# Main-loop matmuls of an attention block issued as pairs of 64-row halves with swapped PSUM banks

## The chip, the cores and the metric

The kernel runs on one core of a Trainium2 chip. The metric is device time in microseconds (us), the median of several executions. The profile of a kernel is one execution; "L426" is line 426 of that kernel, so that the same code has other line numbers in the changed kernel. Engines: PE is TensorE's matmul, PEld its weight load, DVE is VectorE, ACT ScalarE. PSUM is the memory that TensorE writes its results to; "evacuation" is their copying out of it by DVE or ACT. Matmul ends are modelled and some matmul records are missing (15,453 of them beside 15,729 weight loads in the page before the change), so I work with start-to-start times of matmuls that are both there.

## The reference

```python
x = A_x                                   # 2048 x 640, bf16
xn = layernorm(x)
q = (xn @ wq) -> 32 heads of 192          # per head 2048 x 192
scores = q @ k_cache^T * 192**-0.5        # 2048 x 2048 per head
o = softmax(scores) @ v_cache             # 2048 x 192 per head
s = concat(o) @ wo                        # 2048 x 640
g = silu(swiglu(xn, w1, w3, w2))
return x + s * g
```

## The kernel before

It records its operations in program order, finds the dependencies from named keys, and emits each engine's list with semaphore waits. After LayerNorm, the gated MLP and the first Q projection comes the main loop: 512 steps `n`, one for each head `h`, 512 queries `c` and quarter `qd` of the keys. A step computes scores S for 512 keys, takes their exp, multiplies the previous step's result P by V (PV, summed up as O), and in most steps does one "filler": a piece of the Q projection for the next pair of heads, or of the output projection Wo for the last pair. A head's 192 features are split into 128 (`KT0`, `QT0`) and 64 (`KT1`, `QT1`); the 64-row matmuls of even and odd keys use different halves of the array's rows (in the trace the two start 3 to 4 ns apart).

PSUM is four slots of two banks. `O_ps` is slot 3; S takes two of the other three slots, the filler the third, in rotation. The code is shortened; `...` stands for what is cut.

```python
def emit_S(h, c, qd):
    ss = [slot(), slot()]
    for jj in range(2):
        for par in range(2):            # 128 rows
            matmul(ps[ss[jj]][:, par*512:(par+1)*512], KT0[:, hs, par, ...], QT0[:, q4, ...], start=True, stop=False)
    for jj in range(2):
        for par in range(2):            # 64 rows
            rows = slice(64 * par, 64 * par + 64)
            matmul(ps[ss[jj]][:, par*512:(par+1)*512], KT1[rows, hs, par, ...], QT1[rows, q4, ...], start=False, stop=True)

def emit_PV(h, c, qd):                  # 128 rows, 16 matmuls of 193 columns
    for t in range(4):
        for kk in range(4):
            matmul(O_ps[:, t, 0:193], P_sb[:, pb, jj, par, t*128:(t+1)*128], V_sb[:, hs, 2*qd+jj, par, 0:193], ...)

def qproj1(m, c, engs=("dve",), nrot=3):        # the 64 last features of two heads: "second part"
    s = slot(nrot)
    ...                                          # five 128-row matmuls into ps[s][:, 0:512]
    for hh in range(2):
        for half in range(2):                    # each 64 rows twice, for both halves of the array
            evac_copy(engs[hh % len(engs)], QT1[64*half:64*half+64, h % 4, c*512:(c+1)*512],
                      dst[64*hh:64*hh+64, :], ...)
...
for n in range(total):
    emit_S(h, c, qd); emit_exp(h, c, qd)
    if n >= 1:
        emit_PV(...)                             # of step n - 1
        if k % 4 == 3: unit_tail(k // 4)         # O: reciprocal and scaling on DVE
    for fn in fl[i]: fn()                        # filler
```

## Time and profile before

Median 2116.6 us (2115.5 to 2117.9, 4 runs). From the page of the profile: the span, the busy time of PE (us, share of the span, instructions), and the chain of work that ended last.

```profile
span 2115.0 us, 34282 instructions
...
PE 2028.4 (96%) x15453; PEld 1192.0 (56%) x15729; DVE 714.2 (34%) x1301; ACT 1061.0 (50%) x1128; POOL 126.9 (6%) x155
...
PE 94%; DVE 2%; DMA 2%; issue 1%; ACT 1%; SPq 0%; another core or an unknown queue 0%; DVEq 0%
```

TensorE is the bottleneck by all of these lines. What it does with its time stands in the groups of the page: line, engine, operation, names, shape, count, then busy us and mean ns of one.

```profile
L455 PE MATMUL ps<-V_sb,P_sb 128*128 128x193 bf16 x8192 | 771.7, 248 | 0.0
L426 PE MATMUL ps<-QT,KT 128*128 128x512 bf16 x2030 | 522.7, 379 | 3.1 <-ACT P_sb L444 1.2
L385 DVE CAST QT<-ps 64x512 bf16<-64x512 f32 x368 | 253.7, 689 | 616.2 <-PE ps L392 396.6
L434 PE MATMUL ps<-QT,KT 64*128 64x512 bf16 x2048 | 310.1, 381 | 0.0
```

The L385 group mixes shapes: 248 of its 368 copies have 64 rows, 120 have 128. The mean ns is the life of one matmul, and lives overlap. The records of single matmuls show the rate: where nothing holds them up, 512-column matmuls start every 216 ns and 193-column ones every 83 ns. One step in order of time (start us, us, engine, line; brackets give the idle time before and what ended it), first PE, then the weight loads:

```profile
1000.30 1.03 PE L426 MATMUL ps<-QT,KT 128*128 128x512 bf16 x4
1001.26 0.60 PE L434 MATMUL ps<-QT,KT 64*128 64x512 bf16 x4
1001.80 1.51 PE L455 MATMUL ps<-V_sb,P_sb 128*128 128x193 bf16 x16
```

```profile
1001.26 0.11 PEld L434 LDWEIGHTS ps<-QT,KT 64*128 64x128 bf16 x4 [0.42 <-issue]
1001.79 1.28 PEld L455 LDWEIGHTS ps<-V_sb,P_sb 128*128 128x128 bf16 x16 [0.42 <-issue]
```

Four 128-row matmuls should be followed after 4 x 0.216 = 0.86 us; the 64-row ones come after 0.96. Two 64-row pairs should take 0.43 us; PV comes after 0.54. And the loads (94 ns each for the 64-row matmuls, 98 for PV), which elsewhere are hidden under the matmul before, stand still until then. The waits view has it in total (engine, line, what it waited for: us in total, times, longest us):

```profile
PEld ps L434 <- issue: 217.0, 512, 0.4
PEld ps L455 <- issue: 165.0, 389, 0.4
...
PEld ps L485 <- DVE QT L385: 15.5, 56, 0.3
PE ps L485 <- DVE rall L468: 15.4, 56, 0.3
```

The totals are idle time of the weight load, about 0.42 us each; TensorE itself loses 96 and 93 ns. Of the loads of L455, 122 more stand under DVE's names in this view, 109 of them with 46.2 us; the matmuls there are late by the same amount.

### The profile page before, as it was taken

The page shows a single profiled execution, that of the slowest core. Times are in us where ns is not written, and L with a number is a line of the kernel's source. Part 1 is how long each engine was busy: PE and PEld are TensorE (multiplying, and loading weights), DVE is VectorE, ACT ScalarE, POOL GpSimd, SP SyncE. Part 2 cuts the span into 40 slices and gives each one's busy share as a digit, 9 for nine tenths or more (in the row PEclk, how much of TensorE's full clock was granted, in tenths as well). Part 3 has the DMA queues.
Part 4 walks back from the last instruction along what each step waited for, and adds up shares of the span by engine and source line. Part 5 has one row for each costly group of instructions (what it writes and reads, how often), then busy time and mean ns, then how long its engine had stood idle before and what let it go on. Part 6 is the DMA issues. An engine that isn't in the chain of part 4 may idle for free.

```text
span 2115.0 us, 34282 instructions
## 1 busy us (share of the span) xinstructions
PE 2028.4 (96%) x15453; PEld 1192.0 (56%) x15729; DVE 714.2 (34%) x1301; ACT 1061.0 (50%) x1128; POOL 126.9 (6%) x155
## 2 busy tenths in 40 slices
PE   4899999999999999999999999999999999999995
PEld 2444555555555555555555555555555655555563
DVE  4321223333333333333332333323333233332335
ACT  3322655555555555555555555555555555555552
POOL 2000100010101000010101000010101010000000
PEclk9999999999999999999999999999999999999998
DMA  9000032232313222232323112232323222222313
GB/s 235 10 1 1 25 70 50 51 69 43 77 36 71 34 42 58 51 69 43 77 39 82 36 42 43 52 68 51 69 43 77 36 57 43 44 52 51 72 24 96
DMA packets 260586, 115.70 MB, mean 55 GB/s; under 512 B 238544, under 2 KB 250320, under 8 KB 260432
## 3 DMA queue, kind: packets, MB, share of 16 engines
q1 hardware_dynamic: 247488, 70.54, 17.6%
q0 software_dynamic: 12944, 42.87, 7.6%
q8 instruction: 125, 2.05, 0.4%
q14 instruction: 29, 0.24, 0.0%
HBM read 52.04 MB, written 2.62 MB: 26 GB/s over the span
## 4 chain that ended last, share of the span: by engine, by line
PE 94%; DVE 2%; DMA 2%; issue 1%; ACT 1%; SPq 0%; another core or an unknown queue 0%; DVEq 0%
PE ps L455 34%; PE ps L426 21%; PE ps L434 13%; PE ps L485 9%; PE ps L392 6%; PE ps L357 5%; PE ps L403 3%; PE ps L373 2%; DMA w_sb<-in_B_w_dram 1%; DMA x_sb<-in_A_x_dram 1%; DVE rall L468 1%; DVE fin_sb L500 0%; DVE s_acc L493 0%; PE ps L340 0%; DVE o_sb L503 0%
## 5 line engine op out<-in xcount | busy, mean ns | idle before, releaser
L444 ACT ACTIVATE P_sb<-ps 128x1024 bf16<-128x1024 f32 x1024 | 992.3, 1021 | 871.0 <-PE ps L434 870.9
L455 PEld LDWEIGHTS ps<-V_sb,P_sb 128*128 128x128 bf16 x8192 | 655.7, 98 | 216.8 <-issue 165.0
L455 PE MATMUL ps<-V_sb,P_sb 128*128 128x193 bf16 x8192 | 771.7, 248 | 0.0
L426 PE MATMUL ps<-QT,KT 128*128 128x512 bf16 x2030 | 522.7, 379 | 3.1 <-ACT P_sb L444 1.2
L385 DVE CAST QT<-ps 64x512 bf16<-64x512 f32 x368 | 253.7, 689 | 616.2 <-PE ps L392 396.6
L493 DVE TENSOR_TENSOR s_acc<-s_acc,ps 128x640 f32<-128x640 f32 x240 | 196.5, 819 | 487.7 <-PE ps L485 484.9
L434 PE MATMUL ps<-QT,KT 64*128 64x512 bf16 x2048 | 310.1, 381 | 0.0
L426 PEld LDWEIGHTS ps<-QT,KT 128*128 128x128 bf16 x2048 | 188.3, 98 | 195.9 <-ACT P_sb L444 1.7
L485 PE MATMUL ps<-wo_sb,OT_sb 128*128 128x128 bf16 (+1 forms) x1298 | 200.1, 286 | 26.4 <-DVE rall L468 15.4
L434 PEld LDWEIGHTS ps<-QT,KT 64*128 64x128 bf16 x2048 | 58.3, 94 | 217.0 <-issue 217.0
L485 PEld LDWEIGHTS ps<-wo_sb,OT_sb 128*128 128x128 bf16 x1536 | 121.5, 98 | 78.9 <-DVE QT L385 15.5
L392 PE MATMUL ps<-xnT,wq_sb 128*128 128x512 bf16 x639 | 158.5, 379 | 0.1
L470 DVE TENSOR_TENSOR O_sb<-ps,rall 128x384 bf16<-128x384 f32 x256 | 142.8, 558 | 9.1 <-DVE rall L468 0.3
L357 PE MATMUL ps<-xnT,w_sb 128*128 128x512 bf16 x470 | 111.1, 396 | 8.9 <-DMA w_sb<-in_B_w_dram 8.4
L289 POOL DMA_DIRECT2D V_sb<-in_A_v_cache_dram x64 | 56.7, 890 | 876.4 <-PE ps L455 876.4
L392 PEld LDWEIGHTS ps<-xnT,wq_sb 128*128 128x128 bf16 x640 | 60.8, 98 | 47.1
L357 PEld LDWEIGHTS ps<-xnT,w_sb 128*128 128x128 bf16 x480 | 48.2, 101 | 68.7 <-issue 12.8
L403 PE MATMUL ps<-xnT,wq_sb 128*128 128x512 bf16 x319 | 79.5, 379 | 0.1
L468 DVE RECIPROCAL rall<-ps 128x2 f32<-128x2 f32 x256 | 42.3, 165 | 103.3 <-PE ps L455 101.4
L364 DVE TENSOR_TENSOR hT_sb<-sil_sb,ps 128x512 bf16<-128x512 bf16 x48 | 32.7, 681 | 122.9 <-ACT sil_sb L362 122.9
L362 ACT ACTIVATE sil_sb<-ps 128x512 bf16<-128x512 f32 x48 | 28.7, 597 | 86.3 <-PE ps L357 81.3
L283 POOL DMA_DIRECT2D wo_sb<-in_A_wo_dram x16 | 12.3, 766 | 706.2 <-PE ps L485 706.2
(40 smaller groups left out, 290.2 us busy)
## 6 DMA issues: line engine op xcount, KB each, us to landing
V_sb<-in_A_v_cache_dram POOLq DMA_DIRECT2D x64, 384.0 KB, 4.9
wo_sb<-in_A_wo_dram POOLq DMA_DIRECT2D x16, 480.0 KB, 4.2
wq_sb<-in_A_wq_dram POOLq DMA_DIRECT2D x32, 160.0 KB, 3.6
w_sb<-in_B_w_dram SPq DMA_DIRECT2D x8, 480.0 KB, 11.5
x_sb<-in_A_x_dram SPq DMA_DIRECT2D x16, 160.0 KB, 4.9
wq_sb<-in_A_wq_dram POOLq DMA_DIRECT2D x32, 80.0 KB, 3.5
x_sb<-in_A_x_dram SPq DMA_DIRECT2D x4, 640.0 KB, 5.2
out_dram<-o_sb SPq DMA_DIRECT2D x16, 160.0 KB, 1.8
```

The source lines that it names most:

```text
L357: op("pe", lambda e, ct=ct, dst=dst, wt=wt: e.matmul(dst, wt[:, ct, ft * P:(ft + 1) * P], xnT[:, ct, qc * 512:(qc + 1) * 512], start=(ct = ...
L385: op("dve", lambda e: e.tensor_copy(dst, src), r=r, **{mode: w})
L392: op("pe", lambda e, ct=ct: e.matmul(dst, wq_sb[:, m % 2, ct, hh * P:(hh + 1) * P], xnT[:, ct, c * 512:(c + 1) * 512], start=(ct == 0), st ...
L403: op("pe", lambda e, ct=ct: e.matmul(dst, wq_sb[:, m % 2, ct, 2 * P:3 * P], xnT[:, ct, c * 512:(c + 1) * 512], start=(ct == 0), stop=(ct = ...
L426: op("pe", lambda e, jj=jj, j=j, par=par: e.matmul(ps[ss[jj]][:, par * 512:(par + 1) * 512], KT0[:, hs, par, j * P:(j + 1) * P], QT0[:, q4 ...
L434: op("pe", lambda e, jj=jj, j=j, par=par, rows=rows: e.matmul(ps[ss[jj]][:, par * 512:(par + 1) * 512], KT1[rows, hs, par, j * P:(j + 1) * P],
L444: op("act", lambda e, jj=jj, s=s: e.activation(P_sb[:, pb, jj, :, :], ps[s][:, :].rearrange("p (a b) -> p a b", a=2), ACT.Exp, scale=scale ...
L455: op("pe", lambda e, t=t, kk=kk, jj=jj, par=par, first=first: e.matmul(O_ps[:, t, 0:Dh + 1], P_sb[:, pb, jj, par, t * P:(t + 1) * P], V_sb ...
L468: op("dve", lambda e, rr=rr, t0=t0: e.reciprocal(rr, O_ps[:, t0:t0 + 2, Dh:Dh + 1]), r=[("O", b)], w=[("rall", b)])
L470: op("dve", lambda e, rr=rr, t0=t0: e.tensor_tensor(O_sb[:, c, t0:t0 + 2, hh * Dh:(hh + 1) * Dh], O_ps[:, t0:t0 + 2, 0:Dh], rr.to_broadcas ...
L485: op("pe", lambda e, f=f, a=a, b=b: e.matmul(ps[s][:, a:b], OT_sb[:, c, t * 3 + f, :], wo_sb[:, m % 2, f, a:b], start=(f == 0), stop=(f == ...
L493: op("dve", lambda e: e.tensor_tensor(s_acc[:, qt, :], s_acc[:, qt, :], ps[s][:, 0:D], op=ALU.add), r=skeys(s) + [("acc", qt)], w=[("acc", ...
```

## The change

Every main-loop matmul becomes two of 64 rows, one in each half of the array's rows (`k` = 0, 1). The two halves of a pair run at the same time and write different banks `b`; in a second phase they swap banks, so that each bank gets both halves. The intent is to do away with the changes between 128-row and 64-row matmuls. So that both halves never write one bank at once, a recorded dependency makes TensorE wait on its own semaphore before a half writes a bank that the other half wrote last. To give these waits time, the phases of S, PV and filler are interleaved. A second-part Q job now covers 1024 queries, and Q jobs may span two steps, after a fixed pattern.

```diff
+        if tile is not None:
+            bank, k = tile
+            d = self.last_in_bank.get((bank, 1 - k))
+            if d is not None:
+                deps[d.pos] = d
+            self.last_in_bank[(bank, k)] = o
...
-        def qproj0(...)
-        def qproj1(...)
+        def q_phase(kind, m, c, s, phase):
+            for ct in range(NCT):
+                for k in range(2):
+                    b = k if phase == 0 else 1 - k
+                    matmul(ps[s][:, b*512:(b+1)*512], wq_sb[hrows(k), ...], xnT[hrows(k), ct, cc*512:(cc+1)*512],
+                           start=first, stop=..., tile=((s, b), k))
+        def q_evac(kind, m, c, s, engs=("dve", "dve")):
+            ...
+                    evac_copy(engs[hh], QT1[hrows(half), h4 + hh, c * 512:(c + 2) * 512], ps[s][hrows(hh), :], ...)
...
+            for par0 in range(2):            # S, pairs 1 to 4
+                for jj in range(2):
+                    steps.append([(jj, par0, KT0, QT0, 0, par0 == 0), (jj, 1 - par0, KT0, QT0, 1, par0 == 0)])
             for jj in range(2):              # S, pairs 5 and 6
+                steps.append([(jj, 0, KT1, QT1, 0, False), (jj, 1, KT1, QT1, 1, False)])
...
+        PATTERN = "W01WW01WW01.WW.W"         # W: Wo job, 0 and 1: phases of a Q job, '.': no filler
...
-            emit_S(h, c, qd)
-            emit_exp(h, c, qd)
-                emit_PV(...)
-            for fn in fl[i]: fn()
+            steps = emit_S(h, c, qd)
+            cut = 6 if (f1[i] or n == 0) else 4
+            for st in steps[:cut]: st()
+            if cut == 6: emit_exp(h, c, qd)
+            emit_PV(..., 0)                  # first phase
+            for st in steps[cut:]: st()
+            if cut < 6: emit_exp(h, c, qd)
+            if f1[i]: f1[i]()
+            emit_PV(..., 1)                  # second phase, then O's evacuation
+            if f2[i]: f2[i]()
```

(Wo goes the same way, with 320 columns in each bank instead of 512 and 128.)

More of the change, by code (lines that the diff above doesn't have):

```diff
@@ L42, in __init__ @@
         self.dma_cnt = {}
+        self.last_in_bank = {}
     def _key(self, k):
@@ L47, in _key, with op @@
         return self.keys[k]
-    def op(self, eng, fn, r=(), w=(), a=(), dma=None, branch=False):
+    def op(self, eng, fn, r=(), w=(), a=(), dma=None, branch=False, tile=None):
         o = _Op()
@@ L385, in evac_copy, with hrows @@
                 op("dve", lambda e: e.tensor_copy(dst, src), r=r, **{mode: w})
-        def qproj0(h, c, engs=("dve",), nrot=3):
-            s = slot(nrot)
-            m, hh = h // 2, h % 2
-            dst = ps[s][:, 0:512]
+        def hrows(k):
+            return slice(64 * k, 64 * k + 64)
+        def q_phase(kind, m, c, s, phase):
             for ct in range(NCT):
-                op("pe", lambda e, ct=ct: e.matmul(
-                    dst, wq_sb[:, m % 2, ct, hh * P:(hh + 1) * P], xnT[:, ct, c * 512:(c + 1) * 512],
-                    start=(ct == 0), stop=(ct == NCT - 1)),
-                    r=[("wq", m % 2, hh)] + [("xnT", c * 4 + i) for i in range(4)],
-                    **{"w" if ct == 0 else "a": skeys(s)})
-            evac_copy(engs[0], QT0[:, h % 4, c * 512:(c + 1) * 512], dst, skeys(s), [("QT0", h % 4, c)])
@@ L399, in qproj1 @@
-        def qproj1(m, c, engs=("dve",), nrot=3):
-            s = slot(nrot)
-            dst = ps[s][:, 0:512]
-            for ct in range(NCT):
-                op("pe", lambda e, ct=ct: e.matmul(
-                    dst, wq_sb[:, m % 2, ct, 2 * P:3 * P], xnT[:, ct, c * 512:(c + 1) * 512],
-                    start=(ct == 0), stop=(ct == NCT - 1)),
-                    r=[("wq", m % 2, 2), ("wq", m % 2, 3)] + [("xnT", c * 4 + i) for i in range(4)],
-                    **{"w" if ct == 0 else "a": skeys(s)})
-            for hh in range(2):
-                h = 2 * m + hh
-                for half in range(2):
-                    evac_copy(engs[hh % len(engs)], QT1[64 * half:64 * half + 64, h % 4, c * 512:(c + 1) * 512],
-                              dst[64 * hh:64 * hh + 64, :], skeys(s), [("QT1", h % 4, c)],
-                              "w" if half == 0 else "a")
+                for k in range(2):
+                    b = k if phase == 0 else 1 - k
+                    col, cc = (b * P, c) if kind == 0 else (2 * P, c + b)
+                    wk = [("wq", m % 2, b)] if kind == 0 else [("wq", m % 2, 2), ("wq", m % 2, 3)]
+                    first = phase == 0 and ct == 0
+                    op("pe", lambda e, ct=ct, k=k, b=b, col=col, cc=cc, first=first: e.matmul(
+                        ps[s][:, b * 512:(b + 1) * 512], wq_sb[hrows(k), m % 2, ct, col:col + P],
+                        xnT[hrows(k), ct, cc * 512:(cc + 1) * 512],
+                        start=first, stop=(phase == 1 and ct == NCT - 1), skip_group_check=True),
+                        r=wk + [("xnT", cc * 4 + i) for i in range(4)], tile=((s, b), k),
+                        **{"w" if (first and k == 0) else "a": skeys(s)})
@@ new lines, in q_evac @@
+        def q_evac(kind, m, c, s, engs=("dve", "dve")):
+            h4 = 2 * m % 4
+            if kind == 0:
+                for hh in range(2):
+                    evac_copy(engs[hh], QT0[:, h4 + hh, c * 512:(c + 1) * 512], ps[s][:, hh * 512:(hh + 1) * 512],
+                              skeys(s), [("QT0", h4 + hh, c)])
+            else:
+                for hh in range(2):
+                    for half in range(2):
+                        op_r = skeys(s)
+                        evac_copy(engs[hh], QT1[hrows(half), h4 + hh, c * 512:(c + 2) * 512],
+                                  ps[s][hrows(hh), :], op_r,
+                                  [("QT1", h4 + hh, c), ("QT1", h4 + hh, c + 1)], "w" if half == 0 else "a")
@@ L422, in emit_S, with run @@
             hs, q4 = h % 2, h % 4
+            steps = []
+            for par0 in range(2):
+                for jj in range(2):
+                    steps.append([(jj, par0, KT0, QT0, 0, par0 == 0), (jj, 1 - par0, KT0, QT0, 1, par0 == 0)])
             for jj in range(2):
-                j = 2 * qd + jj
-                for par in range(2):
-                    op("pe", lambda e, jj=jj, j=j, par=par: e.matmul(
-                        ps[ss[jj]][:, par * 512:(par + 1) * 512], KT0[:, hs, par, j * P:(j + 1) * P],
-                        QT0[:, q4, c * 512:(c + 1) * 512], start=True, stop=False),
-                        r=[("KT", hs, par), ("QT0", q4, c)], **{"w" if par == 0 else "a": skeys(ss[jj])})
-            for jj in range(2):
-                j = 2 * qd + jj
-                for par in range(2):
-                    rows = slice(64 * par, 64 * par + 64)
-                    op("pe", lambda e, jj=jj, j=j, par=par, rows=rows: e.matmul(
-                        ps[ss[jj]][:, par * 512:(par + 1) * 512], KT1[rows, hs, par, j * P:(j + 1) * P],
-                        QT1[rows, q4, c * 512:(c + 1) * 512], start=False, stop=True),
-                        r=[("KT", hs, 2 + par), ("QT1", q4, c)], a=skeys(ss[jj]))
+                steps.append([(jj, 0, KT1, QT1, 0, False), (jj, 1, KT1, QT1, 1, False)])
+            def run(step):
+                for jj, par, kt, qt, k, first in step:
+                    j = 2 * qd + jj
+                    part = par + (2 if kt is KT1 else 0)
+                    op("pe", lambda e, jj=jj, j=j, par=par, kt=kt, qt=qt, k=k, first=first: e.matmul(
+                        ps[ss[jj]][:, par * 512:(par + 1) * 512], kt[hrows(k), hs, par, j * P:(j + 1) * P],
+                        qt[hrows(k), q4, c * 512:(c + 1) * 512], start=first, stop=kt is KT1,
+                        skip_group_check=True),
+                        r=[("KT", hs, part), ("QT0" if kt is KT0 else "QT1", q4, c)], tile=((ss[jj], par), k),
+                        **{"w" if (first and k == 0) else "a": skeys(ss[jj])})
+            return [lambda st=st: run(st) for st in steps]
         def emit_exp(h, c, qd):
@@ L446, in emit_exp, with emit_PV @@
                     r=skeys(s), w=[("P", pb, jj)])
-        def emit_PV(h, c, qd):
+        def emit_PV(h, c, qd, phase):
             n = (h * NC + c) * NQD + qd
             pb, hs = n % NPB, h % 2
-            for t in range(4):
-                for kk in range(4):
-                    jj, par = kk // 2, kk % 2
-                    first = qd == 0 and kk == 0 and t % 2 == 0
-                    op("pe", lambda e, t=t, kk=kk, jj=jj, par=par, first=first: e.matmul(
-                        O_ps[:, t, 0:Dh + 1], P_sb[:, pb, jj, par, t * P:(t + 1) * P],
-                        V_sb[:, hs, 2 * qd + jj, par, 0:Dh + 1],
-                        start=first, stop=(qd == NQD - 1 and kk == 3), skip_group_check=True),
-                        r=[("P", pb, jj), ("V", hs, par), ("Vones", hs)],
-                        **{"w" if first else "a": [("O", t // 2)]})
+            for kk in range(4):
+                jj, par = kk // 2, kk % 2
+                for tt in range(2):
+                    for k in range(2):
+                        t = 2 * (k if phase == 0 else 1 - k) + tt
+                        first = qd == 0 and phase == 0 and kk == 0 and tt == 0
+                        op("pe", lambda e, t=t, jj=jj, par=par, k=k, first=first: e.matmul(
+                            O_ps[:, t, 0:Dh + 1], P_sb[hrows(k), pb, jj, par, t * P:(t + 1) * P],
+                            V_sb[hrows(k), hs, 2 * qd + jj, par, 0:Dh + 1],
+                            start=first, stop=(qd == NQD - 1 and phase == 1 and kk == 3), skip_group_check=True),
+                            r=[("P", pb, jj), ("V", hs, par), ("Vones", hs)], tile=((3, t // 2), k),
+                            **{"w" if first else "a": [("O", t // 2)]})
         def emit_Oevac(h, c):
@@ L478, in emit_OT, with wo_phase @@
                 r=[("Osb", c)], w=[("OT", c)], dma=f"ot{c}")
-        def emit_Wo(m, c, t):
-            s = slot()
-            qt = c * 4 + t
-            for f in range(3):
-                for a, b in ((0, 512), (512, D)):
-                    op("pe", lambda e, f=f, a=a, b=b: e.matmul(
-                        ps[s][:, a:b], OT_sb[:, c, t * 3 + f, :], wo_sb[:, m % 2, f, a:b],
-                        start=(f == 0), stop=(f == 2)),
-                        r=[("OT", c), ("wo", m % 2)], **{"w" if (f == 0 and a == 0) else "a": skeys(s)})
+        def wo_phase(m, c, t, s, phase):
+            for f in range(3):
+                for k in range(2):
+                    b = k if phase == 0 else 1 - k
+                    first = phase == 0 and f == 0
+                    op("pe", lambda e, f=f, k=k, b=b, first=first: e.matmul(
+                        ps[s][:, b * 512:b * 512 + 320], OT_sb[hrows(k), c, t * 3 + f, :],
+                        wo_sb[hrows(k), m % 2, f, b * 320:(b + 1) * 320],
+                        start=first, stop=(phase == 1 and f == 2), skip_group_check=True),
+                        r=[("OT", c), ("wo", m % 2)], tile=((s, b), k), **{"w" if (first and k == 0) else "a": skeys(s)})
@@ L489, in emit_Wo, with wo_evac @@
+        def wo_evac(m, c, t, s):
+            qt = c * 4 + t
+            acc = s_acc[:, qt, :].rearrange("p (b x) -> p b x", b=2)
+            src = ps[s][:, :].rearrange("p (b x) -> p b x", b=2)[:, :, 0:320]
             if m == 0:
-                op("dve", lambda e: e.tensor_copy(s_acc[:, qt, :], ps[s][:, 0:D]),
-                   r=skeys(s), w=[("acc", qt)])
-            else:
-                op("dve", lambda e: e.tensor_tensor(
-                    s_acc[:, qt, :], s_acc[:, qt, :], ps[s][:, 0:D], op=ALU.add),
-                    r=skeys(s) + [("acc", qt)], w=[("acc", qt)])
+                op("dve", lambda e: e.tensor_copy(acc, src), r=skeys(s), w=[("acc", qt)])
+            else:
+                op("dve", lambda e: e.tensor_tensor(acc, acc, src, op=ALU.add),
+                   r=skeys(s) + [("acc", qt)], w=[("acc", qt)])
@@ new lines, in bass_recurrent_scan__mha_block_cached__glu_gated_swiglu__prompt_kernel, with __init__, p1, p2 @@
+        class Job:
+            def __init__(self, phase, evac, nrot=3):
+                self.phase, self.evac, self.nrot = phase, evac, nrot
+            def p1(self):
+                self.s = slot(self.nrot)
+                self.phase(self.s, 0)
+            def p2(self):
+                self.phase(self.s, 1)
+                self.evac(self.s)
+        def q_job(kind, m, c, engs=("dve", "dve"), nrot=3):
+            return Job(lambda s, ph: q_phase(kind, m, c, s, ph), lambda s: q_evac(kind, m, c, s, engs), nrot)
@@ L497, in emit_final, with wo_job, evac, run_jobs @@
+        def wo_job(m, c, t, then=None):
+            def evac(s):
+                wo_evac(m, c, t, s)
+                if then:
+                    then()
+            return Job(lambda s, ph: wo_phase(m, c, t, s, ph), evac)
+        def run_jobs(jobs):
+            for i in range(0, len(jobs), 2):
+                for j in jobs[i:i + 2]:
+                    j.p1()
+                for j in jobs[i:i + 2]:
+                    j.p2()
         def emit_final(c, t):
@@ L552, in bass_recurrent_scan__mha_block_cached__glu_gated_swiglu__prompt_kernel, with filler_plan, second @@
                 down(qc, qi)
-        for c in range(NC):
-            qproj0(0, c, ("act",), 4)
-            qproj1(0, c, ("dve", "act"), 4)
-            qproj0(1, c, ("act",), 4)
+        run_jobs([q_job(kind, 0, c, ("dve", "act"), 4) for kind, c in ((0, 0), (1, 0), (0, 1), (0, 2), (1, 2), (0, 3))])
         rot[0] = 0
-        fillers = []
         total = H * NC * NQD
-        wo_ready = {}
-        def filler_list(m):
-            f = {i: [] for i in range(32)}
-            if m + 1 < NP:
-                qs = []
-                for c in range(NC):
-                    qs.append(lambda c=c: qproj0(2 * m + 2, c))
-                    qs.append(lambda c=c: qproj1(m + 1, c))
-                    qs.append(lambda c=c: qproj0(2 * m + 3, c))
-                spots = [i for i in range(1, 32, 2) if i % 4 != 1] + [i for i in range(1, 32, 8)]
-                for i, fn in zip(sorted(spots), qs):
-                    f[i].append(fn)
-            if m >= 1:
-                step = 2 if m + 1 < NP else 1
-                for k in range(16):
-                    f[k * step + (2 if step == 1 else 0)].append(lambda k=k: emit_Wo(m - 1, k // 4, k % 4))
-            return f
+        PATTERN = "W01WW01WW01.WW.W"
+        def filler_plan(m):
+            wos = [wo_job(m - 1, k // 4, k % 4) for k in range(16)] if m else []
+            qs = [q_job(kind, m + 1, c) for kind, c in
+                  ((0, 0), (0, 1), (1, 0), (0, 2), (0, 3), (1, 2))] if m + 1 < NP else []
+            f1, f2 = [None] * 32, [None] * 32
+            for i in range(32):
+                ch = PATTERN[i % 16]
+                if m + 1 == NP:
+                    ch = "W" if i < 16 else "."
+                if ch == "W" and wos:
+                    j = wos.pop(0)
+                    f1[i], f2[i] = j.p1, j.p2
+                elif ch == "0" and qs:
+                    f1[i] = qs[0].p1
+                elif ch == "1" and qs:
+                    j = qs.pop(0)
+                    def second(j=j):
+                        assert slot() == j.s
+                        j.p2()
+                    f1[i] = second
+            assert not wos and not qs
+            return f1, f2
         def unit_tail(u):
@@ L588, in bass_recurrent_scan__mha_block_cached__glu_gated_swiglu__prompt_kernel, with last_job, then @@
         tail_q = []
+        def last_job(cc, t):
+            def then():
+                emit_final(cc, t)
+                if t == 3 and cc < 3:
+                    load_x2(cc + 1)
+            return wo_job(NP - 1, cc, t, then)
         for n in range(total):
@@ L592, in bass_recurrent_scan__mha_block_cached__glu_gated_swiglu__prompt_kernel @@
             if i == 0:
-                fl = filler_list(m)
+                f1, f2 = filler_plan(m)
                 load_wo(m)
@@ L596, in bass_recurrent_scan__mha_block_cached__glu_gated_swiglu__prompt_kernel @@
                     load_wq(m + 2)
-            emit_S(h, c, qd)
-            emit_exp(h, c, qd)
-            if n >= 1:
-                k = n - 1
-                emit_PV(k // 16, (k // 4) % 4, k % 4)
+            if tail_q and tail_q[0][0] <= n and f1[i] is None:
+                j = last_job(*tail_q.pop(0)[1:])
+                f1[i], f2[i] = j.p1, j.p2
+            steps = emit_S(h, c, qd)
+            cut = 6 if (f1[i] or n == 0) else 4
+            for st in steps[:cut]:
+                st()
+            if cut == 6:
+                emit_exp(h, c, qd)
+            k = n - 1
+            if n >= 1:
+                emit_PV(k // 16, (k // 4) % 4, k % 4, 0)
+            for st in steps[cut:]:
+                st()
+            if cut < 6:
+                emit_exp(h, c, qd)
+            if f1[i]:
+                f1[i]()
+            if n >= 1:
+                emit_PV(k // 16, (k // 4) % 4, k % 4, 1)
                 if k % 4 == 3:
@@ L607, in bass_recurrent_scan__mha_block_cached__glu_gated_swiglu__prompt_kernel @@
                             tail_q.append((n + 2, cc, t))
-            for fn in fl[i]:
-                fn()
-            if tail_q and tail_q[0][0] <= n:
-                _, cc, t = tail_q.pop(0)
-                emit_Wo(m, cc, t)
-                emit_final(cc, t)
-                if t == 3 and cc < 3:
-                    load_x2(cc + 1)
+            if f2[i]:
+                f2[i]()
             if n % 16 == 1 and h + 1 < H:
@@ L622, in bass_recurrent_scan__mha_block_cached__glu_gated_swiglu__prompt_kernel @@
         k = total - 1
-        emit_PV(k // 16, (k // 4) % 4, k % 4)
+        j = last_job(*tail_q.pop(0)[1:])
+        emit_PV(k // 16, (k // 4) % 4, k % 4, 0)
+        j.p1()
+        emit_PV(k // 16, (k // 4) % 4, k % 4, 1)
         unit_tail(k // 4)
+        j.p2()
         for t in range(4):
@@ L639, in bass_recurrent_scan__mha_block_cached__glu_gated_swiglu__prompt_kernel @@
         op("dve", lambda e: e.tensor_copy(flag[:], ps[s][0:1, 0:1]), r=skeys(s), w=["flag"])
-        for (_, cc, t) in tail_q:
-            emit_Wo(NP - 1, cc, t)
-            emit_final(cc, t)
-            if t == 3 and cc < 3:
-                load_x2(cc + 1)
+        run_jobs([last_job(cc, t) for (_, cc, t) in tail_q])
         for e in ENGS:
@@ L703, in bass_recurrent_scan__mha_block_cached__glu_gated_swiglu__prompt_kernel @@
                 load_wo(m)
-                for c in range(NC):
-                    qproj0(h, c)
-                    qproj1(m, c)
-                    qproj0(h + 1, c)
+                run_jobs([q_job(kind, m, c) for kind, c in ((0, 0), (1, 0), (0, 1), (0, 2), (1, 2), (0, 3))])
             for part in range(4):
@@ L715, in bass_recurrent_scan__mha_block_cached__glu_gated_swiglu__prompt_kernel @@
                     emit_OT(c)
-                    if m == NP - 1:
+                    if m == NP - 1 and c == 0:
                         load_x2(c)
-                    for t in range(4):
-                        emit_Wo(m, c, t)
-                        if m == NP - 1:
-                            emit_final(c, t)
+                    run_jobs([last_job(c, t) if m == NP - 1 else wo_job(m, c, t) for t in range(4)])
         finals_safe = {"sp": [(f"out{i}", S.dma_cnt[f"out{i}"]) for i in range(2)]}
```

## The prediction

> **What bounds it now.** TensorE: the page gives it 96% busy and 94% of the chain that ended last; granted clock 0.993. ACT (50%) and DVE (34%) have room. In the main loop (218 to 2081 us, 512 steps, 3.64 us each) the records of single matmuls show it streams: 128x512 starts every 216 ns, PV's 128x193 every 83 ns, weight loads (98 ns) hidden. Semaphore waits hardly stop it.
>
> **What the change can win.** Each step changes row size twice: 128-row to 64-row scores takes 312 ns start to start instead of 216, 64-row scores to PV 308 ns after a matmul that streams 216. That is 96 + 93 = 189 ns, 512 times: 97 us. In the waits view it is the "issue" time before the L434 and L455 loads. [...] Column counts stay: two halves start 3 ns apart today and the next pair 226 ns after the first, as for a lone matmul after a stall. So I expect pairs at 216 (512 columns) and 83 ns (193).
>
> **What it adds** (estimates from trace durations):
> 1. Waits of TensorE on itself. A 512 matmul signals 393 ns after its start; a waiting load starts 42 ns later: 435 ns, against 432 for the pairs up to there. With the exposed load (+10 ns) a tight wait costs about 17 ns, twice per step: 18 us in all. PV and filler waits: about 0.
> 2. The second-part Q job. Its evacuation becomes four 64x1024 DVE copies. 64x512 takes 688 ns, so 1.22 us each, 4.9 us. The PSUM slot is wanted by the scores two steps on, about 3.5 us after the job's last matmul; the copies end at about 5.3 us. TensorE idles about 1.8 us, 2 x 15 times: 54 us. Today no such stall.
> 3. O evacuation (1.43 us) starts only when both banks finish; scores plus Wo just cover it, but the Wo addition behind it (0.82 us) holds its slot about 0.12 us too long: about 15 us. Without Wo filler (first and last head pair) O itself stalls 0.8 us some 9 times: 7 us.
> 4. Steps without filler run their exps later, 0.18 us some 45 times: 9 us.
> 5. PE instructions double (31,000 to about 60,000): 118 per step, 30 ns each on average, 21 ns inside PV; today's densest stretch is 41 ns. No trace here shows a limit; I assume none binds.
>
> Sum: 2117 - 97 + 18 + 54 + 15 + 7 + 9 = 2123 us, all on the critical path, since TensorE is. Predicted 2120 us, 8 in 10 between 2070 and 2190. Faster by over 2%: 0.14; within 2%: 0.63; slower by over 2%: 0.23.
>
> **What would show it.** Right: the "issue" gaps gone; pairs at 216 and 83 ns; TensorE idle about 1.8 us after each second-part Q job, released by the DVE copy to QT1; small s_pe waits before the third and fifth score pair. Wrong: PV pairs slower than 83 ns (loads or instruction rate bind); waits on TensorE's own semaphore costing some 100 ns; no stall after the 64x1024 copies.
>
> **What would make it wrong.** PV pairs at 95 ns instead of 83 would add 98 us: clearly slower. If 1024-column copies are cheaper than I scale, or the slot is free in time, 54 us fall away: 2 to 3% faster. [...] hence the waits, and if they cost much more than 17 ns each (over 1,000), the gain goes.

Its sum came to 2123 us, rounded to 2120. That the -97 us are gained when the row size no longer changes was the author's estimate, which run 1 tests.

## The result and the profile after

2095.2 us (2094.4 to 2096.7, 4 runs) against 2116.6 us: ratio 0.990, 95% interval 0.988 to 0.992. The page of the changed kernel:

```profile
span 2092.9 us, 59902 instructions
...
PE 1976.1 (94%) x28465; PEld 1266.1 (60%) x28465; DVE 686.4 (33%) x1181; ACT 1058.0 (51%) x1120; POOL 126.8 (6%) x155
...
PE 88%; DVE 9%; DMA 2%; ACT 0%; issue 0%; SPq 0%; DVEq 0%
```

DVE has come up in the chain from 2% to 9%. The groups, the copies by form (each shape apart):

```profile
L475 PE MATMUL ps<-V_sb,P_sb 64*128 64x193 bf16 x16384 | 852.4, 243 | 3.3 <-issue 1.9
L448 PE MATMUL ps<-QT,KT 64*128 64x512 bf16 x6144 | 793.3, 380 | 55.0 <-DVE QT L393 51.7
```

```profile
L393 DVE CAST QT<-ps 64x1024 bf16<-64x1024 f32 x124 | 151.5, 1222 | 158.8 <-PE ps L407 157.5
```

A copy of 1024 columns takes 1222 ns, as scaled in the prediction. The waits view:

```profile
PEld ps L448 <- PE ps L448: 174.0, 513, 0.3
...
PEld ps L448 <- DVE QT L393: 58.1, 30, 1.9
PE ps L448 <- DVE QT L393: 51.7, 31, 1.7
...
PEld ps L448 <- ACT P_sb L461: 20.6, 52, 1.2
```

The "issue" lines of S and PV loads are gone, but for a single wait of 2.1 us. One step in order of time, to set beside that of the kernel before:

```profile
967.94 1.51 PE L448 MATMUL ps<-QT,KT 64*128 64x512 bf16 x12
969.28 0.83 PE L475 MATMUL ps<-V_sb,P_sb 64*128 64x193 bf16 x16
```

Six pairs should take 6 x 0.216 = 1.30 us; PV comes after 1.34. In place of the "issue" lines stand waits of loads on PE itself (TensorE's own semaphore), and 30 waits of the scores for DVE's copies to QT1. One of these in order of time:

```profile
947.34 3.70 DVE L393 CAST QT<-ps 64x1024 bf16<-64x1024 f32 x3
...
948.56 0.83 PE L475 MATMUL ps<-V_sb,P_sb 64*128 64x193 bf16 x16
...
951.10 0.11 PEld L448 LDWEIGHTS ps<-QT,KT 64*128 64x128 bf16 x4 [1.94 <-DVE QT L393]
951.10 1.52 PE L448 MATMUL ps<-QT,KT 64*128 64x512 bf16 x12 [1.71 <-DVE QT L393]
```

The copies end at 951.04 and the scores, which want the same slot, start at once.

From the records of single matmuls I made a ledger of the main loop: each start-to-start time, less the undisturbed one of that size (two halves that start 3 to 4 ns apart count as one pair; undisturbed pairs start every 216, 136 and 83 ns for 512, 320 and 193 columns, just as single 128-row matmuls of 512 and 193 do before).

| us lost by TensorE in the main loop | before | after |
|---|---|---|
| change of row size: 512 x (96 + 93 ns), and 10 ns more for the first matmul after each | 108 | 0 |
| slot held by the copies to QT1 | 13 (56 Wo jobs and 4 scores, 0.22 each) | 56 (30 x 1.87) |
| "tight" waits, on TensorE's own semaphore within S, which other work doesn't quite cover (10 to 13 ns each, up to four in a step) | 0 | 20 |
| slot held by an exp (52 x 0.18) | 0 | 9 |
| the rest (O's evacuation about 2; one gap of 2.0 us whose releaser the profile doesn't show; unsorted) | 2 | 11 |
| sum | 123 | 96 |
| length of the loop, first to last score matmul | 1863.4 | 1838.7 |

For each row but "the rest", there is an experiment below.

### The profile page after: what moved, and what is told of

It reads as the page before. It is cut to its first block, busy times and chain, and to the rows that moved or that the text cites. A ratio compares the mean times of both kernels' runs of the same rounds, so it can differ in the third digit from the quotient of the medians.

```text
span 2092.9 us, 59902 instructions
## 1 busy us (share of the span) xinstructions
PE 1976.1 (94%) x28465; PEld 1266.1 (60%) x28465; DVE 686.4 (33%) x1181; ACT 1058.0 (51%) x1120; POOL 126.8 (6%) x155
## 4 chain that ended last, share of the span: by engine, by line
PE 88%; DVE 9%; DMA 2%; ACT 0%; issue 0%; SPq 0%; DVEq 0%
PE ps L448 31%; PE ps L475 30%; PE ps L407 10%; PE ps L505 10%; DVE QT L393 7%; PE ps L365 5%; PE ps L381 2%; DMA w_sb<-in_B_w_dram 1%; DMA x_sb<-in_A_x_dram 0%; DVE fin_sb L554 0%; DVE O_sb L490 0%; PE ps L348 0%; DVE s_acc L518 0%; DMA OT_sb<-O_sb 0%; DVE o_sb L557 0%
## 5 line engine op out<-in xcount | busy, mean ns | idle before, releaser
L475 PE MATMUL ps<-V_sb,P_sb 64*128 64x193 bf16 x16384 | 852.4, 243 | 3.3 <-issue 1.9
L448 PE MATMUL ps<-QT,KT 64*128 64x512 bf16 x6144 | 793.3, 380 | 55.0 <-DVE QT L393 51.7
L475 PEld LDWEIGHTS ps<-V_sb,P_sb 64*128 64x128 bf16 x16384 | 719.4, 94 | 137.2 <-DVE O_sb L490 3.6
L448 PEld LDWEIGHTS ps<-QT,KT 64*128 64x128 bf16 x6144 | 288.2, 93 | 443.3 <-PE ps L448 174.0
L393 DVE CAST QT<-ps 128x512 bf16<-128x512 f32 (+1 forms) x248 | 231.6, 954 | 487.6 <-PE ps L407 486.4
L505 PE MATMUL ps<-wo_sb,OT_sb 64*128 64x320 bf16 x3072 | 293.2, 297 | 1.2 <-DVE s_acc L518 0.7
L407 PE MATMUL ps<-xnT,wq_sb 64*128 64x512 bf16 x1920 | 238.1, 377 | 0.0
L505 PEld LDWEIGHTS ps<-wo_sb,OT_sb 64*128 64x128 bf16 x3072 | 140.6, 94 | 25.7 <-DVE s_acc L518 1.3
L407 PEld LDWEIGHTS ps<-xnT,wq_sb 64*128 64x128 bf16 x1920 | 86.8, 94 | 75.8 <-issue 0.3
L381 PE MATMUL ps<-w_sb,hT_sb 128*128 128x512 bf16 (+1 forms) x384 | 52.8, 299 | 0.0
```

The costliest lines, as they stand in the source:

```text
L381: op("pe", lambda e, ft=ft, a=a, b=b: e.matmul(ps[s][:, a:b], hT_sb[:, ft, qi * P:(qi + 1) * P], w2_sb[:, ft, a:b], start=(ft == 0), stop= ...
L393: op("dve", lambda e: e.tensor_copy(dst, src), r=r, **{mode: w})
L407: op("pe", lambda e, ct=ct, k=k, b=b, col=col, cc=cc, first=first: e.matmul(ps[s][:, b * 512:(b + 1) * 512], wq_sb[hrows(k), m % 2, ct, co ...
L448: op("pe", lambda e, jj=jj, j=j, par=par, kt=kt, qt=qt, k=k, first=first: e.matmul(ps[ss[jj]][:, par * 512:(par + 1) * 512], kt[hrows(k), ...
L475: op("pe", lambda e, t=t, jj=jj, par=par, k=k, first=first: e.matmul(O_ps[:, t, 0:Dh + 1], P_sb[hrows(k), pb, jj, par, t * P:(t + 1) * P], ...
L505: op("pe", lambda e, f=f, k=k, b=b, first=first: e.matmul(ps[s][:, b * 512:b * 512 + 320], OT_sb[hrows(k), c, t * 3 + f, :], wo_sb[hrows(k ...
```

## The experiments

### 1. The price of changing the row size

Before tells of 96 and 93 ns at the changes, but not that the change is their cause. In this run the 64-row matmuls of the kernel before take all 128 rows. The sums are wrong; the comparison with the reference passed all the same, so passing says little about these sums.

```diff
-                    rows = slice(64 * par, 64 * par + 64)
+                    rows = slice(0, P)
```

> The kernel before with its four 64-row score matmuls of each step made 128-row ones (wrong result on purpose, the sums take rows that don't belong). They can then no longer run two at a time, so they stream 4 x 216 instead of 2 x 216 ns: +432 ns a step, +221 us. Theory A, the 96 + 93 ns and the 10 ns after each are the price of changing the row size: they go too, about -209 ns a step, -107 us, so about 2230 us. Rival B, the gaps belong to something else at these places (second tile of K, first use of P): they stay, about 2337 us.

Measured: 2214.3 us (4 runs), ratio to before 1.046. One step in order of time:

```profile
1001.50 1.03 PE L426 MATMUL ps<-QT,KT 128*128 128x512 bf16 x4
1002.36 1.03 PE L434 MATMUL ps<-QT,KT 128*128 128x512 bf16 x4
1003.23 1.50 PE L455 MATMUL ps<-V_sb,P_sb 128*128 128x193 bf16 x16
```

Four matmuls are now followed after 0.86 us, at both places: in the ledger both gaps, and the 10 ns after each, are 0. Theory A holds, B falls. The time is 16 us under A's number because the row of the QT1 copies, 13 us, went to 0 too (the longer step gave the copies to QT1 the 0.22 us that they lacked). 2117 + 221 - 108 - 13 = 2217 us, 3 us from the measured time.

### 2. The slot held by the copies to QT1

Two of the four copies go to ACT, which has room (51% busy).

```diff
-                        evac_copy(engs[hh], QT1[hrows(half), ...
+                        evac_copy(("dve", "act")[hh], QT1[hrows(half), ...
```

> The changed kernel with the two copies of the second head of a second-part Q job on ACT instead of DVE. Theory A, the scores two steps on wait for the slot until four 1.22 us copies are through: with two on each engine they end about 2.4 us earlier, the 30 stalls of 1.87 us go: 2095 - 56 = about 2040 us. Rival B, ACT takes the exps later for the two copies and the stall comes back as a wait for P or for the slot of the exps: between 2060 and 2095 us.

Measured: 2043.6 us (5 runs, up to 2048.1), ratio to before 0.966 (0.965 to 0.967). In the waits view the 30 score waits for DVE's copies are gone (one, of 0.4 us, is left):

```profile
PEld ps L448 <- PE ps L448: 172.9, 512, 0.3
PEld ps L448 <- ACT P_sb L461: 32.1, 82, 1.2
```

Theory A, nearly to the number. Of the 56 us, 51 to 52 came: with the big stall gone, the 30 steps show the wait for the exp's slot that it had covered (82 such waits instead of 52, 0.18 us each, so 5 us).

The stall should move with the claim of the slot. In the next run the second-part job is the first of its three, so that another instruction claims the slot, and sooner.

```diff
-                  ((0, 0), (0, 1), (1, 0), (0, 2), (0, 3), (1, 2))]
+                  ((1, 0), (0, 0), (0, 1), (1, 2), (0, 2), (0, 3))]
```

> The changed kernel with the second-part Q job put first of its three, so that not the scores two steps on but the Wo job of the next step wants its slot, about 2.9 us after the job's last matmul instead of 3.5. The same copies, the same work. Theory A (the stall is the end of the copies minus the claim of the slot): stalls of about 2.5 us instead of 1.87, now before the Wo matmuls, +17 us: about 2112 us. Rival B (the cost is DVE time or order, not the slot): no change, 2095 us.

Measured: 2134.6 us (4 runs), ratio to before 1.009. The stalls did what theory A says: 28 of 2.51 us, now before Wo (L505), which doesn't read QT1, so it is the slot that it waits for.

```profile
PEld ps L505 <- DVE QT L393: 72.2, 28, 2.6
```

But the kernel lost 39 us, not 17. Its granted clock was 0.983 to 0.984 in all four runs, against 0.993. Three stretches of its trace, each in us and then with busy time and count per engine, the granted clock (PEclk) third from the end: in the first TensorE stalls from 341.1 to 343.6, the second follows on it, and the third is one long after it, at whose end the next stall begins.

```profile
340.60:344.00 3.40, 1.05 (x22) 0.74 (x20) 2.93 (x3) 1.76 (x2) 0.00 (x0) 0.99 1.04 177
344.00:347.40 3.40, 3.40 (x32) 2.04 (x28) 0.82 (x1) 0.00 (x0) 0.00 (x0) 0.50 0.16 36
398.40:401.80 3.40, 3.23 (x50) 1.92 (x46) 2.77 (x3) 1.58 (x3) 0.00 (x0) 1.00 0.00 0
```

After the stall TensorE runs at half its clock for 3.4 us (0.50; a phase of PV, 16 matmuls from 344.09, takes 1.50 us there instead of the 0.83 from 340.43). The clock record shows this after 12 of the 28 stalls of 2.51 us; what sets these 12 apart from the other 16 stays open. Before and after the change the record has no such spell inside the main loop, so none follows the 30 stalls of 1.87 us. 12 x 3.4 us at half clock lose about 20 us. So 15 us are longer stalls (71 us in the ledger instead of 56), 20 us the clock, and 5 us 80 waits for an exp's slot instead of 52.

To see whether the job's place in itself cost anything, the same order with the split copies:

> The kernel a_part2_first with the QT1 copies split over DVE and ACT. Its 28 stalls of 2.51 us were longer by 15 us in all, but it was 39 us slower; the clock record shows 12 more spells of half clock of 3.4 us, each right after such a stall. Theory A (stall, then throttle): both go with the copies, the job's place costs nothing, about 2044 us and 5 spells of half clock as in a_evac_split. Rival B (part of the 39 us is the order of the jobs): 2055 us or more.

Measured: 2047.8 us (4 runs), ratio to before 0.967; the clock record has its five spells of half clock outside the loop, as the changed kernel has, and none inside. A holds: with the copies split, the stalls and the spells of half clock both went. Of the 4 us that remain to the other order's 2043.6, the trace shows 3.5: 28 Wo jobs still start 0.125 us late.

```profile
PEld ps L505 <- issue: 4.5, 28, 0.2
```

Their loads start 0.115 us after DVE's two copies end, all 28 alike. That the slot held them is likely but not shown, since the view names no releaser.

### 3. The same wait in the kernel before

The ledger shows 13 us in the kernel before that I had not counted: 56 Wo jobs (my expectation says 57) and 4 scores that start 0.22 us late. The waits view named two DVE operations. The edit splits the copies there too:

```diff
-                    qs.append(lambda c=c: qproj1(m + 1, c))
+                    qs.append(lambda c=c: qproj1(m + 1, c, ("dve", "act")))
```

> The kernel before, in its main loop, with the two copies of the second head of a second-part Q projection on ACT instead of DVE. In its trace 57 of the Wo jobs start some 0.22 us late, 13 us in all. Theory A, which the prediction had not seen: those wait for the slot that four QT1 copies of 0.69 us hold, so the waits go: about 2103 us. Rival B, they wait for the O evacuation that stands before them on DVE: they stay, 2116 us.

Measured: 2102.9 us (5 runs) against 2116.9 in the same rounds, ratio 0.994 (0.992 to 0.995). The row-size lines stay, the 56 waits of L485 for QT are gone:

```profile
PEld ps L434 <- issue: 217.0, 512, 0.4
PEld ps L455 <- issue: 166.5, 393, 0.4
...
PEld ps L485 <- DVE s_acc L493: 1.7, 2, 1.5
```

So the kernel before had this fault in a small form. The change took those 13 us away and put 56 us in another place.

### 4. Waits on TensorE's own semaphore

In S, a pair that swaps banks waits for the pair two places before. Exchanging the second and third pair puts it right behind the one that it waits for.

```diff
+            steps[1], steps[2] = steps[2], steps[1]
```

> The changed kernel with the second and third score pair of a step exchanged: now the pair that swaps the banks comes straight after the one that it waits for. Theory A (a wait on TensorE's own semaphore is 435 ns from the start of the matmul waited for): two waits a step cost 219 + 10 ns each instead of 12; the longer step also gives the copies to QT1 0.45 us more, so their 30 stalls shrink: 2280 to 2315 us. Rival B (the wait is a fixed 10 to 13 ns, wherever it stands): about 2095 us.

Measured: 2296.6 us (4 runs), ratio to before 1.085. In the ledger the pairs two and four of S come 229 ns late (216 + 229 = 445 from the start of the pair waited for), 2 x 117 us in all. The 30 stalls for QT1 shrank from 1.87 to 1.42 us.

```profile
PEld ps L449 <- PE ps L449: 661.1, 1455, 0.6
PEld ps L449 <- DVE QT L393: 44.4, 30, 1.5
```

A holds: in these traces such a wait lasts from the start of a 512-column matmul waited for about 437 ns to the load (394 to the signal, 43 to the load), and costs what is not covered by other work. The order of the changed kernel covers all but 10 to 13 ns, four times a step. A phase of PV (8 pairs, 8 x 83 = 664 ns) between the two, as in the steps without filler, covers it wholly: in the changed kernel's trace a score pair that follows PV starts 83 or 84 ns after PV's last pair in 312 of 342 cases, and the other 30 are the stalls of 1.87 us.

### 5. Steps without filler, and the best version

In steps without filler S's last two pairs stand behind PV's first phase, so their exps begin late. Here only the last pair does.

```diff
-            cut = 6 if (f1[i] or n == 0) else 4
+            cut = 6 if (f1[i] or n == 0) else 5
```

> The changed kernel; in steps without filler the fifth score pair is done before PV's first phase, not after it. Theory A (52 waits of 0.18 us for the slot of the exp are there because the exps of these steps begin 0.67 us late): they go, the wait for the fifth pair becomes a tight one (+13 ns in 80 steps, 1 us): about -8 us, 2087 us. Rival B (ACT itself is late): no change.

Measured: 2087.0 us (4 runs), ratio to before 0.986 (0.985 to 0.988). The 9 us in the ledger's row are 0. In the waits view only one score load still waits for ACT's exps, at the loop's start:

```profile
PEld ps L448 <- ACT P_sb L461: 1.2, 1, 1.2
```

A holds.

Both edits together, and the first six Q jobs (before the loop) in another order, so that their long copies come first:

> The changed kernel with the copies to QT1 split over DVE and ACT, the fifth pair early in steps without filler, and the first Q jobs reordered so that the last two before the loop have short copies. If the three gains are separate: -56, -8 and -2 us, about 2030 us. If they share a cause, nearer 2040 us.

Measured: 2030.8 us (5 runs), ratio to before 0.960 (0.958 to 0.961). The gains add up. The third edit was not run alone; the loop starts 1.8 us sooner than with the split copies alone (218.8 instead of 220.6 us).

```profile
PEld ps L448 <- PE ps L448: 174.8, 513, 0.3
...
PEld ps L448 <- ACT P_sb L461: 1.2, 1, 1.2
```

At last an attempt on the 20 us of tight waits: in three of four filler steps half of PV's first phase goes between S's second and third pair.

```diff
+            spread = cut == 6 and n >= 1 and n % 4 != 1
...
+                if spread and x == 1:
+                    emit_PV(k // 16, (k // 4) % 4, k % 4, 0, (0, 1))
...
-                emit_PV(k // 16, (k // 4) % 4, k % 4, 0)
+                emit_PV(k // 16, (k // 4) % 4, k % 4, 0, (2, 3) if spread else range(4))
```

> The kernel a_best, and in steps with filler (three of four) half of PV's first phase is put between the second and the third score pair, so that the waits before the third and fourth pair are no longer tight. Theory A (a tight wait costs 10 to 13 ns because the load after it is exposed): 24 ns in about 310 steps, -7 us against a_best, if the exps, now 0.33 us later, don't make the scores of the next step wait for their slot. Rival B: that wait costs more than is gained, 0.05 to 0.1 us a step, +10 to +25 us.

Measured: 2027.0 us (5 runs) against 2030.8 in the same rounds; ratio to before 0.958 (0.957 to 0.959).

```profile
PEld ps L448 <- PE ps L448: 156.4, 513, 0.6
PEld ps L448 <- ACT P_sb L461: 53.4, 245, 1.2
```

Both theories have a share. The tight waits are gone in 306 steps (7 us by the ledger), and the later exps give back 3 us: 245 loads wait for them, mostly so shortly that the matmul hardly starts later. 4 us are left, and the intervals of the two versions against before overlap a little. It beats the kernel before by 4.2% and the changed kernel by about 68 us.

## Why the prediction was right, and which of its terms were not

The prediction said 2120 us (2070 to 2190), within 2%. It was 2095. Its sum, 2123 us, has the kernel 6 us slower; it became 21 us faster. So the direction was wrong, and that the number came within 1.2% owes something to luck: errors of 44 us one way and 16 the other partly cancelled. Point by point:

- **The gain of 97 us: right in cause, 11 us too small.** Run 1 shows that both gaps belong to the change of row size. The sum left out the 10 ns by which the first matmul after each gap is slower, though the prediction quotes the 226 ns that show it. 108 us. What TensorE does in these gaps, no trace here shows.
- **Pairs at 216 and 83 ns: right.** Doubling the instructions cost nothing visible: PV goes at four instructions in 83 ns, 21 ns each.
- **Term 1, tight waits, 18 us: right in sum (20), wrong in form.** I expected two waits of 17 ns in a step. There are up to four of 10 to 13. Run 4 confirms the 435 ns behind it (437 measured there).
- **Term 2, the QT1 copies, 54 us: right (56).** Copy 1.22 us, stall 1.87 us, 30 times; run 2 removes it. But the sentence "Today no such stall" was wrong: before had it 60 times at 0.22 us, 56 of them before Wo jobs, as run 3 shows. The lines were in the waits view, and I had taken them for nothing ("Semaphore waits hardly stop it"). The change therefore gained 13 us more than I counted.
- **Term 3, the Wo addition holding its slot, 15 us: wrong, below 1 us.** I had taken the time from O's first reciprocal to the Wo addition, 1.48 us, from a step of before. In the changed kernel's trace it is 1.34 us (967.74 to 969.08), and the addition is through just when the slot is wanted: 84 loads of Q jobs wait for DVE, but their matmuls start about 5 ns late. O itself, without Wo filler: 7 us predicted, about 2 measured.
- **Term 4, late exps, 9 us: right** (52 x 0.18 us). Run 5 removes it.
- **Term 5, no limit from the number of instructions: right**, as the pairs at 83 ns show.
- The rest: the loop starts 1.6 us later and what comes after the last score is 1 us longer. About 7 us of the ledger's "rest" I can't assign.

So the sum of 2123 us was 11 + 13 + 15 + 5 us too high in these terms, and lacked some 16 us of small ones (of which about 7 are the unassigned ones): 28 us between it and the 2095 measured.

That the two halves must not write one bank at once is the author's assumption, and why the waits are there. No run here takes them away, so it was not shown that the chip needs them.

## What to carry to other kernels

If TensorE alternates between 128-row and 64-row matmuls, count the alternations: each change cost some 0.1 us here (96 and 93 ns, and 10 for the first matmul after each), and splitting the 128-row matmuls into pairs of halves was free in streaming (216 and 83 ns, as before). A change that moves whole blocks of work also moves the claims on every PSUM slot; list for each slot when its last reader ends and when its next writer wants it, since three quarters of a gain of 108 us vanished here in waits, most of them of this kind. Read the small lines of the waits view of the kernel before, too: the same fault may already be there.
